# Last block of a two-layer network: the order of the last token tiles' matmuls, and a last store in three parts on two queues

## The chip, the core and the metric

The kernel runs on one core of a Trainium2 chip. The core has five engines that run their own instruction streams and meet at semaphores: TensorE (matmuls, with weight loads of their own), VectorE, ScalarE, GpSimd and SyncE (SP), which only issues transfers and waits. Sixteen DMA engines move data between the on-chip memory SBUF and the device's memory. TensorE writes to PSUM, another on-chip memory, in banks of 2 KB for each of 128 partitions; VectorE and ScalarE read PSUM, and DMA cannot, so a result goes from PSUM through a copy to SBUF and from there by a transfer to the output.

The metric is the device time of one execution in microseconds (us), lower is better. Of the kernel before there are three timed runs, and one more execution that the hardware profiler recorded.

## What is computed

```python
def _attn_ref(x, filt_r, filt_i):            # x: 8 x 3008 x 256
    X = np.fft.rfft(x, axis=1)
    F = (filt_r + 1j * filt_i)[None, :, :]
    y = np.fft.irfft(X * F, n=x.shape[1], axis=1)
    return y.astype(np.float32)

def _moe_ref(x, w_in, w_out, alpha):         # x: 24064 x 256, w_in: 256 x 2048
    h = x @ w_in
    g = np.maximum(h, 0.0) + alpha * np.minimum(h, 0.0)
    return (g @ w_out).astype(np.float32)    # w_out: 2048 x 256
```

A Fourier filter over each of 8 sequences, then for each of the 24064 tokens a network of two layers with a slope per hidden channel for negative values. The output is fp32, 256 values a token.

## The kernel before

The tokens are taken two sequences at a time, 6016 tokens, in twelve blocks of 512 tokens (one of them 384); in all there are 48 blocks. The Fourier work of the next sequences is put between the blocks' matmuls by a plan of steps written out by hand, and it is over before the last blocks, so that the end of the kernel is the two-layer network alone.

For a block, `Block.up` (L416) does the first layer. The hidden width of 2048 is split into 16 inner tiles of 128. For each inner tile two matmuls of 512 columns fill one bank of an `hps` tile in PSUM (L421). After each second inner tile ScalarE copies both to SBUF as fp16 (L427), and VectorE makes the slope in three instructions (L430 twice, L431); the result, `gtb`, is the weight of the second layer.

`Block.down` (L434) does the second layer. The block's 512 tokens are four token tiles of 128. For each token tile 16 matmuls, one for each inner tile `k`, accumulate 128 x 256 results into one half of an `op` tile (one bank of PSUM): the weight is the 128 x 128 piece of `gtb`, the moving operand `wout_s[:, k]`, 256 columns (L440). The token tiles run one after another, `k` from 0 to 15 in each. After every second token tile ScalarE copies both halves to an `osb` tile in SBUF (L445), and `store` (L395) issues a transfer from SP for each token tile, one part or two parts, because the tokens lie in the output in groups of 376 that the Fourier step has reordered (L403). The three `osb` tiles are used in turn, the two `op` tiles and the two `hps` tiles likewise.

The main loop (L511 to L520) runs the blocks with a lag: while block n does its first layer, four second-layer matmuls of block n - 1 follow each inner tile. After the loop the last block's second layer stands alone (L521, L522): 64 matmuls, in the order token tile 0 with `k` 0 to 15, then token tiles 1, 2 and 3. The last pair of inner tiles, `k` 14 and 15, comes from the last first-layer matmuls, through ScalarE and VectorE. In the last block token tile 0 is stored in one transfer, token tile 1 in two, token tiles 2 and 3 in one each.

Every transfer that SP and ScalarE issue uses one of eight semaphores in turn. At the end SP waits for each of them, and then the engines meet at a barrier.

Of the kernel before, what the change touches and what calls it, by code (L numbers as in the profile page):

```python
# [11 lines left out]
FP32 = mybir.dt.float32  # L12
# [3 lines left out]
N2 = 64  # L16
NK1 = 24
D = 256
# [14 lines left out]
AF = mybir.ActivationFunctionType  # L33
# [42 lines left out]
def kernel(  # L76
# [10 lines left out]
    nc = tc.nc  # L87
# [16 lines left out]
    p_osb = ctx.enter_context(tc.tile_pool(name="p_osb", bufs=3))  # L104
    psH = ctx.enter_context(tc.tile_pool(name="psH", bufs=2, space=bass.MemoryType.PSUM))
    psO = ctx.enter_context(tc.tile_pool(name="psO", bufs=2, space=bass.MemoryType.PSUM))
# [18 lines left out]
    wout_s = konst.tile([128, 16, D], FP16, name="wout_s")  # L125
# [215 lines left out]
    for q in range(2):  # L341
        nc.gpsimd.dma_start(
            out=wout_s[:, 8 * q : 8 * q + 8],
            in_=moe_w_out[1024 * q : 1024 * q + 1024].rearrange("(j p) d -> p j d", p=128))
# [44 lines left out]
    for p in range(NB // 2):  # L389
        t = 0  # L390
# [1 line left out]
            blocks.append((p, t, tn, 2 * p + (n >= 6)))  # L392
            t += tn

    def store(p, t0, osb, lane):  # L395
        t = t0
        while t < t0 + 128:
            b, r = 2 * p + t // NFFT, t % NFFT
            blk, o = r // 376, r % 376
            n = min(t0 + 128 - t, 376 - o)  # L400
            g, h = blk // 2, blk % 2
            row = b * NFFT + (o // 8) * N2 + NH * h + 8 * g
            nc.sync.dma_start(  # L403
                out=bass.AP(tensor=out.tensor, offset=out.offset + row * D,
                            ap=[[N2 * D, n // 8], [D, 8], [1, D]]),
                in_=osb[t - t0 : t - t0 + n, lane])
            t += n

    turn = [0]
# [1 line left out]
    class Block:  # L411
# [22 lines left out]
        def down(self, q):  # L434
            n = self.tn // 128
            for w in range(n * q, n * (q + 1)):
                si, k = w // 16, w % 16
                if si % 2 == 0 and k == 0:
                    self.op = psO.tile([128, 2, D], FP32, name="op")
                nc.tensor.matmul(self.op[:, si % 2], self.gts[k][:, 128 * si : 128 * si + 128],  # L440
                                 wout_s[:, k], start=(k == 0), stop=(k == 15))
                if k == 15 and (si % 2 == 1 or si == n - 1):
                    m = si % 2 + 1
                    osb = p_osb.tile([128, 2, D], FP32, name="osb")
                    nc.scalar.activation(osb[:, 0:m], self.op[:, 0:m], AF.Copy)  # L445
                    for lane in range(m):
                        store(self.p, self.t0 + 128 * (si - m + 1 + lane), osb, lane)

    plan = {}

# [37 lines left out]
    for b in range(3, NB):  # L488
        p = 96 * (b - 1)
# [19 lines left out]
    prev = None  # L509
    step = 0  # L510
    for p, t0, tn, _ in blocks:  # L511
# [6 lines left out]
                prev.down(j)  # L518
            step += 1
        prev = blk  # L520
    for q in range(16):  # L521
        prev.down(q)  # L522
    assert not plan


# [28 lines left out]
```

## Time and profile before

| what | value |
|---|---|
| timed runs, median of 3 | 797.27 us (796.84 to 797.43) |
| profiled execution, its time | 795.65 us |
| its span, first to last record | 793.9 us |
| TensorE busy in the span | 775.0 us, 98% |
| ScalarE, VectorE busy | 75%, 78% |
| DMA engines, mean share of the two data queues | 32.9% and 24.3% |
| granted TensorE clock, mean | 0.999 |

In the profile's lines an engine's name stands for its own work (PE is TensorE, PEld its weight loads, DVE VectorE, ACT ScalarE, POOL GpSimd, SP SyncE), and a q behind it for its queue, where it issues a transfer or waits. `out<-in` names what is written and read by the program's names, and L440 is a line of the kernel. A group's line has the count behind an x, then busy time and the mean of one in ns, then the idle time before, with what ended most of it. A timeline's line has the start and the length in us, and instructions of one line that follow each other stand together. Matmuls are pipelined: each is recorded with its whole way through the array, so that neighbours overlap, and the spacing of their starts is what one costs in a row. A transfer's issue is recorded on the queue of the engine that issues it; its landing is what a later wait is released by.

### The profile page before, as it was taken

How to read it: one execution, taken by the hardware profiler on the slowest of the kernel's cores; microseconds unless marked ns; L12 is line 12 of the kernel's file. 1: busy time of each engine (PE TensorE's matmuls, PEld its weight loads, DVE VectorE, ACT ScalarE, POOL GpSimd, SP SyncE). 2: the span in 40 equal slices, each digit the busy share in tenths (PEclk: the TensorE clock that was granted, in tenths of full speed). 3: DMA queues.
4: the chain of work that ended last, by engine and by line, in shares of the span. 5: the costliest groups of instructions: out<-in, count | busy, mean ns of one | idle time of the engine just before them, and what ended most of it. 6: DMA issues, size and time to landing. Idle time of an engine off the chain costs nothing.

```text
span 793.9 us, 16103 instructions
## 1 busy us (share of the span) xinstructions
PE 775.0 (98%) x5956; PEld 538.5 (68%) x5956; DVE 621.2 (78%) x1377; ACT 596.9 (75%) x836; POOL 193.2 (24%) x269
## 2 busy tenths in 40 slices
PE   7999999999999999999999999999999999999997
PEld 6756656666677666766667666766667766766665
DVE  4797985788788787888787877887878888777773
ACT  3788678878778887788768887688867777787663
POOL 7510441153123221341223311242212222000000
PEclk9999999999999999999999999999999999999999
DMA  9967557695776648574684657656494333511111
GB/s 187 209 142 194 115 112 175 192 180 118 150 173 113 138 102 192 123 147 101 149 189 82 135 120 167 152 109 139 101 212 90 66 77 81 138 36 28 41 40 54
DMA packets 102310, 100.58 MB, mean 127 GB/s; under 512 B 11320, under 2 KB 92744, under 8 KB 102104
## 3 DMA queue, kind: packets, MB, share of 16 engines
q1 hardware_dynamic: 79512, 68.80, 32.9%
q0 software_dynamic: 22720, 30.75, 24.3%
q8 instruction: 47, 0.77, 0.4%
q14 instruction: 31, 0.25, 0.1%
HBM read 56.26 MB, written 46.66 MB: 130 GB/s over the span
## 4 chain that ended last, share of the span: by engine, by line
PE 89%; ACT 4%; DMA 3%; DVE 2%; issue 1%; SPq 0%; POOL 0%; ACTq 0%; DVEq 0%; POOLq 0%
PE hps L421 38%; PE op L440 38%; PE psF L177 3%; PE psF L238 3%; ACT gtb L427 2%; PE psF L216 2%; PE psF L197 2%; DMA uu<-ww 1%; DMA filt_s<-in_filt_i_dram 1%; DMA xs<-in_x_dram 1%; ACT asb L245 1%; PE hps L288 1%; PE psF L317 1%; DMA v_dram<-v 0%; DMA zt<-v_dram 0%
## 5 line engine op out<-in xcount | busy, mean ns | idle before, releaser
L427 ACT ACTIVATE gtb<-hps 128x1024 f16<-128x1024 f32 (+1 forms) x384 | 385.4, 1005 | 133.3 <-PE hps L421 127.9
L440 PE MATMUL op<-wout_s,gtb 128*128 128x256 f16 x3008 | 451.1, 272 | 0.6 <-DVE gtb L431 0.6
L421 PE MATMUL hps<-yT,win_s 128*128 128x512 f16 (+1 forms) x1536 | 449.2, 374 | 0.4 <-ACT gtb L427 0.2
L440 PEld LDWEIGHTS <-gtb 128*128 128x128 f16 x3008 | 293.2, 98 | 189.6 <-DVE gtb L431 0.9
L430 DVE TENSOR_SCALAR m<-gtb,alm_s 128x512 f16<-128x512 f16 (+1 forms) x768 | 235.7, 349 | 126.7 <-ACT gtb L427 124.4
L431 DVE TENSOR_TENSOR gtb<-gtb,m 128x1024 f16<-128x1024 f16 (+1 forms) x384 | 261.6, 681 | 19.9
L203 POOL DMA_DIRECT2D uu<-ww x168 | 140.6, 980 | 438.3 <-PE hps L421 322.1
L421 PEld LDWEIGHTS <-win_s 128*128 128x128 f16 x1536 | 145.3, 98 | 30.9 <-issue 3.1
L245 ACT ACTIVATE asb<-psF 96x512 f16<-96x512 f32 x112 | 66.2, 591 | 11.5 <-PE psF L177 11.4
L245 ACT ACTIVATE yT<-psF 128x376 f16<-128x376 f32 x120 | 57.1, 485 | 13.3 <-PE psF L238 12.8
L445 ACT ACTIVATE osb<-op 128x512 f32<-128x512 f32 x96 | 56.1, 585 | 6.1 <-issue 3.2
L245 ACT ACTIVATE v<-psF 128x512 f16<-128x512 f32 x84 | 49.4, 595 | 10.8 <-PE psF L216 10.0
L200 DVE TENSOR_TENSOR ww<-psF,filts_s 128x512 f16<-128x512 f32 x84 | 57.4, 684 | 0.0
L201 DVE TENSOR_TENSOR uu<-psF,filt_s 128x512 f16<-128x512 f32 x84 | 57.2, 681 | 0.0
L139 POOL DMA_DIRECT2D xs<-in_x_dram x64 | 43.9, 946 | 25.8 <-PE psF L177 15.0
L177 PE MATMUL psF<-xs,wf_s 94*96 94x512 f16 x112 | 42.7, 381 | 1.5 <-ACT v L245 1.0
L238 PE MATMUL psF<-wi_s,zt 96*128 96x94 f16 x504 | 40.3, 205 | 1.9 <-DMA zt<-v_dram 1.0
L238 PEld LDWEIGHTS <-zt 96*128 96x128 f16 x512 | 34.3, 97 | 6.2 <-issue 1.5
L216 PE MATMUL psF<-uu,twi_s 128*128 128x256 f16 x168 | 31.3, 273 | 2.3 <-ACT yT L245 0.9
L197 PE MATMUL psF<-at,twf_s 128*128 128x256 f16 x168 | 32.1, 273 | 0.3 <-ACT asb L245 0.2
L216 PEld LDWEIGHTS <-twi_s 128*128 128x128 f16 x168 | 15.7, 98 | 5.9 <-DMA uu<-ww 2.7
L197 PEld LDWEIGHTS <-twf_s 128*128 128x128 f16 x168 | 15.8, 98 | 2.8 <-DVE uu L201 0.7
(55 smaller groups left out, 173.3 us busy)
## 6 DMA issues: line engine op xcount, KB each, us to landing
out_dram<-osb SPq DMA_DIRECT2D x128, 128.0 KB
xs<-in_x_dram POOLq DMA_DIRECT2D x64, 188.0 KB, 5.4
a_dram<-asb SPq DMA_DIRECT2D x28, 384.0 KB
uu<-ww POOLq DMA_DIRECT2D x168, 64.0 KB, 2.9
v_dram<-v SPq DMA_DIRECT2D x112, 96.0 KB
zt<-v_dram SPq DMA_DIRECT2D x28, 384.0 KB
at<-a_dram SPq DMA_DIRECT2D x20, 384.0 KB
at<-a_dram SPq DMA_DIRECT2D x32, 96.0 KB
```

Source lines behind the costliest of these rows:

```text
L177: nc.tensor.matmul(ps[0:96], wf1_s, xs[:, o : o + 512], start=True, stop=True)
L197: nc.tensor.matmul(px[:, kh], twf_s[:, k1], self.at[:, k1], start=True, stop=True)
L200: nc.vector.tensor_mul(ww, px, filts_s[:, 2 * kp : 2 * kp + 2])
L203: nc.gpsimd.dma_start(out=uu[o : o + 64], in_=ww[64 - o : 128 - o], accum_op=OP.add)
L216: nc.tensor.matmul(pv[:, kh], twi_s[:, k1], u[:, kh], start=u is us[0], stop=u is us[-1])
L238: nc.tensor.matmul(ps[:, m], self.zt[:, 8 * g + 4 * mh + m, dh * 128 : dh * 128 + 128], wi3_s, start=True, stop=True)
L245: nc.scalar.activation(o, i, AF.Copy)
L421: nc.tensor.matmul(self.hps[:, j % 2, 0:tn], win_s[:, kt, j * 128 : (j + 1) * 128], yT[:, kt, self.t0 : self.t0 + tn], start=(kt == 0), st ...
L427: nc.scalar.activation(g[:, :, 0:tn], self.hps[:, :, 0:tn], AF.Copy)
L430: nc.vector.tensor_scalar(m[:, i, 0:tn], g[:, i, 0:tn], 0.0, a, OP.min, OP.mult)
L431: nc.vector.tensor_add(g[:, :, 0:tn], g[:, :, 0:tn], m[:, :, 0:tn])
L440: nc.tensor.matmul(self.op[:, si % 2], self.gts[k][:, 128 * si : 128 * si + 128], wout_s[:, k], start=(k == 0), stop=(k == 15))
```

## The change

A method `finish` takes the place of the last block's 16 calls of `down`, and `store` learns to take another queue and a range of columns.

```diff
-    def store(p, t0, osb, lane):
+    def store(p, t0, osb, lane, eng=nc.sync, ca=0, cb=D):
...
-            nc.sync.dma_start(
-                out=bass.AP(tensor=out.tensor, offset=out.offset + row * D,
-                            ap=[[N2 * D, n // 8], [D, 8], [1, D]]),
-                in_=osb[t - t0 : t - t0 + n, lane])
+            eng.dma_start(
+                out=bass.AP(tensor=out.tensor, offset=out.offset + row * D + ca,
+                            ap=[[N2 * D, n // 8], [D, 8], [1, cb - ca]]),
+                in_=osb[t - t0 : t - t0 + n, lane, ca:cb])
...
+        def finish(self):
+            def down(acc, si, k, first, ca=0, cb=D):
+                nc.tensor.matmul(acc, self.gts[k][:, 128 * si : 128 * si + 128], wout_s[:, k, ca:cb],
+                                 start=first, stop=(k == 15), skip_group_check=True)
+
+            op = psO.tile([128, 2, D], FP32, name="op")
+            osb = p_osb.tile([128, 2, D], FP32, name="osb")
+            for ks in (range(14), range(14, 16)):
+                for si in range(2):
+                    for k in ks:
+                        down(op[:, si], si, k, si == 0 and k == 0)
+            nc.scalar.activation(osb, op, AF.Copy)
+            for lane in range(2):
+                store(self.p, self.t0 + 128 * lane, osb, lane)
+            osb = p_osb.tile([128, 2, D], FP32, name="osb")
+            parts = ((0, 0, 256, nc.sync), (1, 0, 128, nc.scalar), (1, 128, 256, nc.sync))
+            accs = [psH.tile([128, 2, 512], FP32, name="hps")[:, 0] for _ in range(2)]
+            accs.insert(0, psO.tile([128, 2, D], FP32, name="op")[:, 0])
+            for (lane, ca, cb, eng), acc in zip(parts, accs):
+                acc = acc[:, 0 : cb - ca]
+                for k in range(16):
+                    down(acc, 2 + lane, k, k == 0, ca, cb)
+                nc.vector.tensor_copy(osb[:, lane, ca:cb], acc)
+                store(self.p, self.t0 + 256 + 128 * lane, osb, lane, eng, ca, cb)
...
-    for q in range(16):
-        prev.down(q)
+    prev.finish()
```

Token tiles 0 and 1 now share the order: `k` 0 to 13 of token tile 0, `k` 0 to 13 of token tile 1, then `k` 14 and 15 of each. ScalarE copies both as before, and SP stores them in three transfers as before. Token tile 2 is accumulated by itself, copied by VectorE and stored from SP. Token tile 3 is done twice over half the columns: 16 matmuls of 128 columns, a copy on VectorE, a store from ScalarE's queue; then the other 16, a copy, a store from SP. The three accumulators lie in an `op` tile and in the two `hps` tiles, which the first layer no longer needs. Each half of token tile 3 loads the 16 weights again.

The program's instructions before the last block's second layer are the same, engine by engine. TensorE has 16 matmuls and 16 weight loads more, VectorE three copies more, ScalarE one copy less and one transfer to issue, and SP's last transfer has half the size.

## The prediction

> **What bounds the kernel now.** I read the page first, its spans and its chain.
>
> ```profile
> span 793.9 us, 16103 instructions
> PE 775.0 (98%) x5956; PEld 538.5 (68%) x5956; DVE 621.2 (78%) x1377; ACT 596.9 (75%) x836; POOL 193.2 (24%) x269
> ...
> PE 89%; ACT 4%; DMA 3%; DVE 2%; issue 1%; SPq 0%; POOL 0%; ACTq 0%; DVEq 0%; POOLq 0%
> ```
>
> TensorE is busy for 98% of the span. The change touches nothing before the last block's second layer, so only the end matters: the last 14 us. I take it from the timeline of that stretch, in windows cut so that single stores stand alone.
>
> ```profile
> 780.49 2.13 PE L440 MATMUL op<-wout_s,gtb 128*128 128x256 f16 x18
> 782.46 0.69 DVE L431 TENSOR_TENSOR gtb<-gtb,m 128x1024 f16<-128x1024 f16 x1
> 782.99 1.51 SPq L403 DMA_DIRECT2D out_dram<-osb  x2
> 783.21 5.63 PE L440 MATMUL op<-wout_s,gtb 128*128 128x256 f16 x50 [0.60 <-DVE gtb L431]
> 785.44 0.60 ACT L445 ACTIVATE osb<-op 128x512 f32<-128x512 f32 x1 [3.24 <-issue]
> 786.06 2.07 SPq L403 DMA_DIRECT2D out_dram<-osb  x3
> 788.93 0.60 ACT L445 ACTIVATE osb<-op 128x512 f32<-128x512 f32 x1 [2.90 <-PE op L440]
> 789.55 0.57 SPq L403 DMA_DIRECT2D out_dram<-osb  x1
> 789.55 1.20 SPq L403 DMA_DIRECT2D out_dram<-osb  x2
> ```
>
> The columns are start, length, engine, line. The 18 matmuls that end at 782.62 are the previous block's last 4 and the first 14 of token tile 0. Matmul 15 needs inner tile 14, whose last VectorE step runs from 782.46 to 783.15. TensorE stands still from 782.62 to 783.21, then does the other 50 in 5.63 us, one each (5.63 - 0.27)/49 = 0.109 us, to 788.84. ScalarE copies token tiles 2 and 3 in one piece (788.93 to 789.53), and SP issues their two stores, the second from 790.2. What follows is in the waits of SP's queue and in the view of line 403:
>
> ```profile
> SPq L549 <- DMA out_dram<-osb: 1.7, 1, 1.7
> ...
> L403 SPq DMA_DIRECT2D out_dram<-osb x248: 447/632/1817, 60.5 to 790.2; - x124
> ```
>
> SP has issued by 789.55 + 1.20 = 790.75 and waits 1.7 us, to about 792.5, for the last store to land: 2.35 us after that store's issue began at 790.17. From there to 793.9 it is closing waits and the barrier, 1.4 us, which stay. So the end is a chain of links: the stall, the matmuls, a copy, two issues in a row, a landing.
>
> **The change part by part.**
>
> *Order of the matmuls.* Token tile 1's first 14 now stand between tile 0's 14 and the two that need the last inner tiles. They take 14 x 0.109 = 1.53 us, so TensorE asks for inner tile 14 at 782.62 + 1.53 = 784.15; it is ready at 783.15. The stall is covered with 1.0 us to spare. Token tiles 0 and 1 end at 782.62 + 18 x 0.109 = 784.59; before, it was 783.21 + 0.27 + 17 x 0.109 = 785.34. Gain **0.75**: the gap of 0.59, and 0.16 because the first matmul after a gap takes its whole 0.27 and not 0.109. Putting both tiles in one bank with one start flag changes no time.
>
> *Half-width matmuls.* Token tile 3's 16 matmuls of 256 columns become 32 of 128, with 16 weight loads more. Nearest rows: 128x128 matmuls with a fresh weight load each, at full clock, and the weight load of this very layer.
>
> ```profile
> 18.43 0.22 PE L306 MATMUL op<-gtb,ww 128*128 128x128 f16 x1 [1.12 <-DVE gtb L355]
> ...
> 18.77 0.22 PE L306 MATMUL op<-gtb,ww 128*128 128x128 f16 x1
> ...
> 33.70 0.61 PE L351 MATMUL op<-id 128*128 128x128 f16 x8
> ...
> L440 PEld LDWEIGHTS <-gtb 128*128 128x128 f16 x3008 | 293.2, 98 | 189.6 <-DVE gtb L431 0.9
> ```
>
> Between 18.43 and 18.77 lie six steps, 0.057 us each; the run of eight gives (0.61 - 0.22)/7 = 0.056. Two halves thus cost 0.112 against 0.109: 16 x 0.003 = 0.05 us lost, and the last, shorter matmul leaves the array 0.05 sooner. I take **0**. The other bound is a load that isn't hidden: 32 x (0.098 - 0.056) = 1.3 us lost. The rows with a load per matmul are the same shape, so I stay with them. TensorE ends at 784.59 + 32 x 0.109 = 788.08 less 0.01.
>
> *The copies.* Before: one ScalarE copy of 0.60, begun 0.09 after TensorE. After: three on VectorE, which has nothing left to do. No row shows this copy; the nearest are VectorE's reads of PSUM.
>
> ```profile
> L248 DVE CAST gtb<-hps 128x384 f16<-128x384 f32 x8 | 4.2, 554 | 10.2 <-PE hps L267 10.1
> L248 DVE CAST at<-psF 128x512 f16<-128x512 f32 x1 | 0.7, 692 | 0.3 <-PE psF L278 0.3
> L364 DVE COPY al_s<-op 128x16 f32<-128x16 f32 x1 | 0.2, 175 | 0.0
> ...
> 14.18 0.80 PE L278 MATMUL psF<-id,gtb 128*128 128x128 f16 x8
> 15.02 0.69 DVE L248 CAST at<-psF 128x512 f16<-128x512 f32 x1 [0.35 <-PE psF L278]
> ```
>
> One more column costs (692 - 554)/128 = 1.08 ns, so 128 columns take 554 - 256 x 1.08 = 278 ns, and 256 take 416. VectorE began 15.02 - 14.98 = 0.04 after TensorE. On the path stands only the last copy: 0.04 + 0.28 = 0.32 instead of 0.09 + 0.60 = 0.69. Gain **0.37**; bounds 0.47 (as short as the 16-column row, 0.175) and 0.23 (as long as 256 columns). The first VectorE copy gains a wait for the stores that read its buffer three turns ago, those of the previous block's token tiles 0 and 1; SP had issued that block's later stores by 784.50, and the copy starts at 786.4. Behind it on VectorE are only the other two copies.
>
> *The issues.* The three stores of tiles 0 and 1 now follow the ScalarE copy that ends at 784.59 + 0.09 + 0.60 = 785.28, take 2.07, and hold SP until 787.36. Tile 2 is copied by 784.59 + 16 x 0.109 + 0.04 + 0.42 = 786.79 but is issued behind them, 787.41 to 787.98. The first half of tile 3 is copied at 787.50 and goes to ScalarE's queue, where nothing stands before or behind it. The second half: TensorE 788.07, copy done 788.39, SP free since 788.03, issue at **788.41**. If the two queues cannot issue at once, three issues in a row, 0.62 apart as the pair at 789.55 shows, put the last at 788.64. I take 788.5. Before it was 790.17: 1.67 us sooner, of which 0.75 is the stall, 0.37 the copy and 0.62 the one issue that no longer stands ahead, less 0.07 for waiting.
>
> The Trainium skill, Perfetto Trace Analysis, section on the HWDGE DMA instruction, says that the descriptor generator is one block, locked by the sequencer that uses it; by that rule the issue is at 788.64, 0.14 later than I take. No row of this trace has two such queues.
>
> *The landing.* The last store is 64 KB in 512-byte pieces, not 128 KB in 1-KB pieces. The views of the DMA engines, in 40 slices, first the two last stores (789.5 to 792.7), then four stores of 96 KB in 512-byte pieces (677 to 679.6):
>
> ```profile
> GB/s 0 0 0 0 0 0 0 0 0 0 0 0 0 0 0 38 141 179 154 218 333 230 244 77 128 141 192 205 282 307 205 141 51 13 0 0 0 0 0 0
> ...
> GB/s 0 0 0 0 0 0 0 0 0 0 0 0 0 32 118 213 228 213 213 173 197 166 166 236 205 205 205 181 213 174 173 221 213 205 221 173 418 182 181 228
> ```
>
> Both run near 200 GB/s, so 512-byte pieces aren't slower per byte, and 64 KB move in 0.33 us instead of 0.65. The landing shortens from 2.35 to **2.03**. Bounds: 2.35 (no gain), and 1.76, the first DMA of the program, 32 KB, issued at 0.75 and awaited by TensorE until 2.51:
>
> ```profile
> 0.75 0.36 SPq L320 DMA_DIRECT2D id<-c_id  x1
> ...
> 2.51 1.78 PE L351 MATMUL op<-id 128*128 128x128 f16 x15 [2.51 <-DMA id<-c_id]
> ```
>
> **The sum.** 1.67 + 0.32 = 1.99; I round down to **1.95 us**, since an interleaved store from the other queue can hold some pieces up. Ends: 1.53 (issue at 788.64, landing 2.35) and 2.35 (issue at 788.41, landing 1.76). The profiled execution itself took 795.65, 1.62 under the median of the timed runs; it becomes 793.70, and the median 797.27 becomes **795.32**, likeliest case's own range 794.8 to 795.8.
>
> **The rivals.**
>
> *Halving saves nothing (chance 0.13).* A store's time may be fixed cost: the first slice with traffic begins at 789.5 + 15 x 0.08 = 790.7, 1.15 us after its issue, and the last ends at 792.2, 0.3 before SP is released. With the landing at 2.35 and the issues strictly one after another, the gain is 1.53: 795.74. Against it: the 0.65 us of traffic per store that the slices show. The Trainium skill, DMA: Bandwidth & Descriptors, Rules for kernel authors, speaks for it: under 64 KB a transfer is mostly overhead, and issuing from several engines saves the time of the issue alone. Here the traffic is 0.65 of the store's 2.35 us, so the row agrees that most is overhead, not that all is.
>
> *A third queue costs outside the span (0.13).* The page knows two queues for data:
>
> ```profile
> q1 hardware_dynamic: 79512, 68.80, 32.9%
> q0 software_dynamic: 22720, 30.75, 24.3%
> ```
>
> Between span and execution lie 795.65 - 793.9 = 1.75 us. If these two queues make that up, a third adds 0.9, and the gain shrinks to 1.05: 796.2. Nothing in the trace says what the 1.75 us are.
>
> *Weight loads pace the half-width matmuls (0.06).* The 1.3 us above come back: 796.6. Against it stand the rows at 0.056; for it, that none is a run of 32.
>
> *Slower: the first store on ScalarE's queue lands late (0.06).* That queue has carried nothing. On the two others the first transfer took 1.76 us (SP) and, on the POOL queue, which the chain shows at the start:
>
> ```profile
> 1.26 2.19 POOL xs L139 x4
> 3.45 6.13 DMA xs<-in_x_dram
> ```
>
> With such 6.1 us after its four issues, the half tile issued at 787.5 to 788.1 lands at 794.2, 1.7 us after the present last landing at 792.5: 799.0. It decides the time from the point where this landing takes over 3 us from issue, and makes the kernel slower from 5.0. Against it: that transfer was 188 KB from memory at the start, beside others; SP's first was as quick as any.
>
> *The change doesn't do what it says:* the stall stays, if the last inner tile came after 784.15. It has 1.0 us of cover; I give that no chance of its own.
>
> **How the numbers follow.** My forecast has 0.62, the rivals 0.13, 0.13, 0.06 and 0.06. About 0.2% (1.6 us) can be told from no change. The forecast passes that line by 0.35 us and its own range crosses it, so I count nine tenths of it as faster and half of the first rival: 0.62. The second and third rivals are within 0.2%, and so is what is left: 0.33. The last gives 0.05 slower. The range runs from 794.7 (gain 2.35, and 0.2 for the scatter of the medians) to 797.0, which takes in the first three rivals.
>
> **What would show it.** After: no wait of TensorE for line 431 at the end; the 32 half-width matmuls at 0.056; copies on VectorE of 0.42, 0.28 and 0.28; SP's last issue near 788.5 counted from the same start, ScalarE's at 787.5; the waits of SP's queue of about 1.4 us behind the last issue; a span near 791.9. Wrong would be the forecast if half-width matmuls run at 0.1, if ScalarE's issue or landing comes last, or if the span is shorter by 2 us and the execution is not.

## The result and the profile after

The changed kernel takes 794.80 us (median of 13 runs, 793.34 to 797.12); the kernel before, run beside it, 796.84 us (13 runs, 795.49 to 799.30). The medians differ by 2.04 us; the ratio taken over all runs is 0.9977, 95% interval 0.9966 to 0.9988, which is 1.8 us or 0.23% less, with 1.0 to 2.7 us in the interval. The profiled execution took 794.64 us, its span is 792.8.

The span fell by 1.1 us only, so the first question is where the two executions differ. The view by windows gives, for each stretch, its length, TensorE's busy time with the number of matmuls, the granted clock, the DMA share and GB/s. Before:

```profile
0.00:200.00 200.00, 187.28 (x1563) 1.00 0.76 162
200.00:780.00 580.00, 579.44 (x4325) 1.00 0.52 116
```

After:

```profile
0.00:200.00 200.00, 187.15 (x1555) 1.00 0.75 161
200.00:780.00 580.00, 579.44 (x4325) 1.00 0.52 116
```

From 200 us on, both run the same 4325 matmuls in the same time. In the first 200 us the changed kernel did eight fewer, which puts everything later by about 1 us, in a stretch where the two programs are the same. So a span compares two openings as well as two endings. The endings are compared by the **tail**: from the end of the last VectorE step of the last block (line 431) to the end of the span. Before it is 793.884 - 783.156 = 10.73 us (the row of that step is in the prediction). After, in the timeline:

```profile
783.56 0.69 DVE L431 TENSOR_TENSOR gtb<-gtb,m 128x1024 f16<-128x1024 f16 x1
783.98 3.44 PE L451 MATMUL op<-wout_s,gtb 128*128 128x256 f16 x30
785.76 0.60 ACT L460 ACTIVATE osb<-op 128x512 f32<-128x512 f32 x1 [2.47 <-issue]
787.26 1.95 PE L451 MATMUL hps<-wout_s,gtb 128*128 128x128 f16 x32
787.46 0.42 DVE L471 COPY osb<-op 128x256 f32<-128x256 f32 x1 [3.21 <-PE op L451]
788.35 0.29 DVE L471 COPY osb<-hps 128x128 f32<-128x128 f32 x1 [0.47 <-PE hps L451]
788.53 0.57 SPq L403 DMA_DIRECT2D out_dram<-osb  x1
788.67 0.65 ACTq L403 DMA_DIRECT2D out_dram<-osb  x1
789.24 0.29 DVE L471 COPY osb<-hps 128x128 f32<-128x128 f32 x1 [0.60 <-PE hps L451]
789.56 0.55 SPq L403 DMA_DIRECT2D out_dram<-osb  x1
...
SPq L573 <- DMA out_dram<-osb: 1.3, 2, 0.9
```

The tail is 792.82 - 784.25 = **8.57 us, 2.16 less**. The matmuls run on through the end of line 431 without a gap; the row of TensorE waiting for it is gone. TensorE ends at 789.21, 4.96 us after that step (before: 5.69). The last copy is done 0.33 after TensorE, not 0.69. The last issue comes 5.31 after the step, not 7.01. The last row is the waits of SP's queue: after its last issue, over at 790.11, SP waits 0.9 us for ScalarE's store and then 0.4 for its own. The landings themselves are in the trace's semaphore records, finer than these rounded waits: the last store has landed by 791.54, 1.98 after the start of its issue (before: 792.54, 2.37 after). Here and below a landing is counted from the start of the issue.

### The profile page after: what moved, and what is told of

Same layout as the page of the kernel before. It is cut to its first block, busy times and chain, and to the rows that moved or that the text cites. A ratio compares the mean times of both kernels' runs of the same rounds, so it can differ in the third digit from the quotient of the medians.

```text
span 792.8 us, 16142 instructions
## 1 busy us (share of the span) xinstructions
PE 775.8 (98%) x5972; PEld 540.2 (68%) x5972; DVE 622.5 (79%) x1380; ACT 596.4 (75%) x835; POOL 193.0 (24%) x269
## 4 chain that ended last, share of the span: by engine, by line
PE 89%; ACT 3%; DMA 3%; DVE 2%; issue 1%; POOL 1%; SPq 0%; ACTq 0%; POOLq 0%
PE hps L421 38%; PE op L440 38%; PE psF L177 3%; PE psF L238 3%; PE psF L216 2%; PE psF L197 2%; ACT gtb L427 2%; DMA xs<-in_x_dram 1%; DMA uu<-ww 1%; PE hps L288 1%; PE op L451 1%; ACT asb L245 1%; DVE m L430 1%; PE psF L317 1%; DVE ww L200 1%
## 5 line engine op out<-in xcount | busy, mean ns | idle before, releaser
L440 PE MATMUL op<-wout_s,gtb 128*128 128x256 f16 x2944 | 444.0, 272 | 0.0
L440 PEld LDWEIGHTS <-gtb 128*128 128x128 f16 x2944 | 287.0, 98 | 188.0
```

## The experiments

All tails are from one profiled execution each; a tail does not contain the opening. How far they scatter can be read from a link that several kernels share: the last 64-KB store, when SP issues it with no other issue running, lands after 1.98, 1.99, 1.99, 1.99 and 2.00 us in five of them. "The changed kernel" is the kernel after.

**Only the new order of token tiles 0 and 1.** Token tiles 2 and 3 are done as before, and the loop over the parts goes:

```diff
-            parts = ((0, 0, 256, nc.sync), (1, 0, 128, nc.scalar), (1, 128, 256, nc.sync))
...
+            op = psO.tile([128, 2, D], FP32, name="op")
+            for lane in range(2):
+                for k in range(16):
+                    down(op[:, lane], 2 + lane, k, k == 0)
+            nc.scalar.activation(osb, op, AF.Copy)
+            for lane in range(2):
+                store(self.p, self.t0 + 256 + 128 * lane, osb, lane)
```

> Only the new order of token tiles 0 and 1; token tiles 2 and 3 as before (one ScalarE copy, two SP stores). Measured by the tail, from the end of the last VectorE step of line 431 to the end of the span: 10.73 us before, 8.57 after. Links add up: the stall and its refill go, 0.73 us, nothing else: tail 10.00, TensorE ends 4.96 after that step instead of 5.69, copy 0.60 and two issues 0.62 apart unchanged. Rival, the stall alone is the gain and the parts give back what they save: tail 8.6. Rival, the stall moves elsewhere (another wait for VectorE): tail 10.7.

Measured, in its timeline (start, length, engine, line):

```profile
784.21 5.84 PE L451 MATMUL op<-wout_s,gtb 128*128 128x256 f16 x52
784.44 0.69 DVE L431 TENSOR_TENSOR gtb<-gtb,m 128x1024 f16<-128x1024 f16 x1
786.64 0.60 ACT L460 ACTIVATE osb<-op 128x512 f32<-128x512 f32 x1 [2.47 <-issue]
790.14 0.60 ACT L468 ACTIVATE osb<-op 128x512 f32<-128x512 f32 x1 [2.90 <-PE op L451]
```

The 52 matmuls run through the end of line 431 in one piece, and TensorE ends 4.92 after it. Tail 795.08 - 785.13 = 9.95, 0.78 less than before, where 0.73 was expected. Its timed ratio, 0.9994 (0.9978 to 1.0009), is too wide to tell 0.78 us (0.1%) from nothing.

**Only the parts and the second queue.** Token tiles 0 and 1 in the old order:

```diff
-            for ks in (range(14), range(14, 16)):
+            for ks in (range(16),):
```

> Only the three parts and the second queue; token tiles 0 and 1 in the old order, one after the other. Links add up: TensorE stalls 0.59 again, and the copy, the issue and the landing keep their gain, 2.16 - 0.73 = 1.43 us: tail 9.30. Rival, the stall alone is the gain: tail 10.7.

```profile
785.51 0.69 DVE L431 TENSOR_TENSOR gtb<-gtb,m 128x1024 f16<-128x1024 f16 x1
786.26 3.89 PE L451 MATMUL op<-wout_s,gtb 128*128 128x256 f16 x34 [0.60 <-DVE gtb L431]
789.98 1.95 PE L451 MATMUL hps<-wout_s,gtb 128*128 128x128 f16 x32
791.97 0.29 DVE L471 COPY osb<-hps 128x128 f32<-128x128 f32 x1 [0.60 <-PE hps L451]
```

In its timeline the wait of 0.60 is back. Tail 795.56 - 786.20 = 9.36, 1.37 less than before (ratio 0.9983, 0.9968 to 0.9998). The two halves of the change give 0.78 and 1.37, together 2.15 of the whole's 2.16: they add up, and neither gives back what the other saves.

**How much cover the stall needs.** Only 3 of token tile 1's matmuls stand ahead of token tile 0's last two:

```diff
-            for ks in (range(14), range(14, 16)):
-                for si in range(2):
-                    for k in ks:
-                        down(op[:, si], si, k, si == 0 and k == 0)
+            for si, ks in ((0, range(14)), (1, range(3)), (0, range(14, 16)), (1, range(3, 16))):
+                for k in ks:
+                    down(op[:, si], si, k, si == 0 and k == 0)
```

> The changed kernel with only 3 of token tile 1's matmuls ahead of token tile 0's last two, instead of 14. Theory, the stall is covered matmul by matmul, 0.109 us each, and 7 would do for all of it: tail 9.36 (without cover) - 3 x 0.109 = 9.03, a wait of 0.27 left before TensorE's next matmul. Rival, any work in between hides it: tail 8.57. Rival, a gap costs the same however short: tail 9.36.

```profile
785.52 0.69 DVE L431 TENSOR_TENSOR gtb<-gtb,m 128x1024 f16<-128x1024 f16 x1
786.27 3.56 PE L451 MATMUL op<-wout_s,gtb 128*128 128x256 f16 x31 [0.27 <-DVE gtb L431]
```

Tail 795.25 - 786.22 = 9.03, and the wait in the timeline is 0.27: both as the theory has it. A stall is paid for in the time of the work put in front of it, 0.109 us a matmul here. At that price some seven matmuls would cover it all; that was not run, and the 14 of the change leave no wait.

**One queue.** The changed kernel with the first half stored from SP:

```diff
-            parts = ((0, 0, 256, nc.sync), (1, 0, 128, nc.scalar), (1, 128, 256, nc.sync))
+            parts = ((0, 0, 256, nc.sync), (1, 0, 128, nc.sync), (1, 128, 256, nc.sync))
```

> The changed kernel, but the first half of token tile 3 is stored from SP too. Links add up: three issues in a row from 4.28 after the last VectorE step, each 0.55 to 0.62, so the last half is issued at 5.50 instead of 5.31: tail 8.77, 0.2 longer. Rival, the second queue already waits for the first one's issue and saves nothing: tail 8.57.

```profile
783.76 0.69 DVE L431 TENSOR_TENSOR gtb<-gtb,m 128x1024 f16<-128x1024 f16 x1
788.56 0.29 DVE L471 COPY osb<-hps 128x128 f32<-128x128 f32 x1 [0.47 <-PE hps L451]
789.45 0.29 DVE L471 COPY osb<-hps 128x128 f32<-128x128 f32 x1 [0.60 <-PE hps L451]
...
788.74 0.57 SPq L403 DMA_DIRECT2D out_dram<-osb  x1
789.40 0.55 SPq L403 DMA_DIRECT2D out_dram<-osb  x1
790.04 0.56 SPq L403 DMA_DIRECT2D out_dram<-osb  x1
```

The last copy is done at 789.74, but SP issues its store only at 790.04, after the two others, 0.65 apart. Tail 793.32 - 784.46 = 8.86, 0.29 longer than with two queues (0.2 expected: three issues follow each other a little slower than I took). So the second queue does save time.

**No halves.** The changed kernel with token tile 3 at full width:

```diff
-            parts = ((0, 0, 256, nc.sync), (1, 0, 128, nc.scalar), (1, 128, 256, nc.sync))
-            accs = [psH.tile([128, 2, 512], FP32, name="hps")[:, 0] for _ in range(2)]
+            parts = ((0, 0, 256, nc.sync), (1, 0, 256, nc.sync))
+            accs = [psH.tile([128, 2, 512], FP32, name="hps")[:, 0] for _ in range(1)]
```

> The changed kernel, but token tile 3 is done at full width: 16 matmuls of 256 columns, one VectorE copy, one SP store of 128 KB. Links add up: the copy takes 0.42 instead of 0.29, the landing 2.35 instead of 1.98, TensorE ends 0.06 sooner: tail 9.0. Rival, a store's time is fixed and halving saves only in the copy: tail 8.65.

```profile
786.64 0.69 DVE L431 TENSOR_TENSOR gtb<-gtb,m 128x1024 f16<-128x1024 f16 x1
792.28 0.42 DVE L471 COPY osb<-hps 128x256 f32<-128x256 f32 x1 [1.32 <-PE hps L451]
792.74 0.55 SPq L403 DMA_DIRECT2D out_dram<-osb  x1
...
SPq L573 <- DMA out_dram<-osb: 1.7, 1, 1.7
```

The last issue comes 5.41 after the step, 0.10 later than with halves, and SP waits 1.7 us for its landing, 2.28 after the issue instead of 1.98. Tail 796.36 - 787.33 = 9.03, 0.46 longer. Of this, 0.10 is the later issue (the copy takes 0.13 longer, and TensorE ends 0.04 sooner) and 0.30 the landing. The last 0.06 is not the halving's: with one transfer fewer the last store has another semaphore, and one closing wait more follows it (below). The tail of 9.0 that was expected came out in part by luck, as the landing was 0.07 shorter than expected and the closing wait, which had not been counted, 0.06 longer. A store's time is not fixed.

**Is ScalarE's queue slow, or was it in the way of SP's?** ScalarE's store in the changed kernel took 0.65 to issue and landed 2.39 after it (788.67 to 791.06); SP's last store took 0.55 and 1.98. Both are 64 KB. First the queues exchanged, then both halves from ScalarE:

```diff
-            parts = ((0, 0, 256, nc.sync), (1, 0, 128, nc.scalar), (1, 128, 256, nc.sync))
+            parts = ((0, 0, 256, nc.sync), (1, 0, 128, nc.sync), (1, 128, 256, nc.scalar))
```

> The changed kernel with the two halves' queues exchanged: first half from SP, last half from ScalarE. In the changed kernel ScalarE's half took 0.65 to issue and 2.39 to land, SP's last half 0.55 and 1.98. Theory, overlap with another issue made it slow: here the last half overlaps SP's issue by 0.15 us only, lands some 2.05 after its issue: tail 8.6 to 8.7. Rival, ScalarE's queue is slower by itself: the last half lands 2.39 after its issue: tail 9.0.

```diff
-            parts = ((0, 0, 256, nc.sync), (1, 0, 128, nc.scalar), (1, 128, 256, nc.sync))
+            parts = ((0, 0, 256, nc.sync), (1, 0, 128, nc.scalar), (1, 128, 256, nc.scalar))
```

> The changed kernel with both halves stored from ScalarE's queue; SP has long issued token tile 2 when the last half comes. Theory, overlap made it slow: the last half is issued alone, 0.55, and lands in 1.98: tail 8.57. Rival, ScalarE's queue is slower by itself: landing 2.39, tail 9.0.

The issues, in the timelines; with the queues exchanged:

```profile
789.24 0.55 SPq L403 DMA_DIRECT2D out_dram<-osb  x1
789.62 0.66 ACTq L403 DMA_DIRECT2D out_dram<-osb  x1
```

and with both halves from ScalarE, after token tile 2 from SP:

```profile
787.43 0.56 SPq L403 DMA_DIRECT2D out_dram<-osb  x1
787.57 0.66 ACTq L403 DMA_DIRECT2D out_dram<-osb  x1
788.46 0.56 ACTq L403 DMA_DIRECT2D out_dram<-osb  x1
```

ScalarE's issue takes 0.65 to 0.66 beside one of SP's and 0.56 alone (788.46). That store, issued alone, lands after 2.01, as SP's do; in the exchanged kernel, with an overlap of 0.17, it lands after 2.10. Tails 8.70 and 8.61, where 9.0 would have shown a slower queue: ScalarE's queue is no slower by itself.

That the overlap is what makes it slow is not shown. The issue is longer by the same 0.1 whether 0.43 or 0.17 of SP's issue is still to run, SP's own issues in these overlaps stay at 0.55 to 0.57, and in every kernel the issue of 0.65 to 0.66 is also the first transfer on ScalarE's queue, while the one of 0.56 is its second. A price of a queue's first use fits as well, and no run has a first issue that stands alone. The landing is 0.4 later behind a 128-KB store issued 0.14 before it, and 0.1 later behind a 64-KB store issued 0.38 before it; whether that arises in the issue or because both stores' data moves at the same time (in the changed kernel ScalarE's pieces from 790.19 to 790.71, the 128-KB store's up to 790.52), these runs do not tell. The first half of token tile 3 has that time to spare.

**The closing waits.** At the end SP waits for eight semaphores one after another. In the changed kernel the last store has the second of them, so that the other six come after it. Six small transfers more at the start move it to the last:

```diff
-    nc.sync.dma_start(out=wi3_s, in_=wi3_d.ap())
+    for r in range(0, 96, 14):
+        nc.sync.dma_start(out=wi3_s[r : min(r + 14, 96)], in_=wi3_d.ap()[r : min(r + 14, 96)])
```

> The changed kernel with the constant wi3_s loaded in seven transfers at the start instead of one, so that the last store falls on the last of the eight semaphores that SP waits for in turn, not on the second. Theory: after the last landing SP now passes six waits fewer, 0.062 us each: tail 8.57 - 0.37 = 8.20. Rival, the closing time is the barrier's and SP's waits lie beside it: tail 8.57.

```profile
783.94 0.69 DVE L432 TENSOR_TENSOR gtb<-gtb,m 128x1024 f16<-128x1024 f16 x1
789.05 0.66 ACTq L404 DMA_DIRECT2D out_dram<-osb  x1
789.62 0.29 DVE L472 COPY osb<-hps 128x128 f32<-128x128 f32 x1 [0.60 <-PE hps L452]
...
SPq L574 <- DMA out_dram<-osb: 0.8, 2, 0.4
```

Its lines stand one further down. Up to the last copy all is where it was (5.68 after the start of the last VectorE step in both kernels). The wait for the landings falls from 1.3 to 0.8, because SP passes the other semaphores before the data is there. Tail 792.86 - 784.63 = 8.23, 0.35 less than the changed kernel. Timed, its ratio to the kernel before is 0.9971 (0.9955 to 0.9988; median 794.41 against 796.24): it beats the kernel before, and the changed one by its tail; the timed runs alone can't tell these two apart. The four timed kernels stand in the order of their tails: the new order alone, the parts alone, the whole change and this one are 0.06, 0.17, 0.23 and 0.29% faster by their ratios, and their tails are shorter by 0.10, 0.17, 0.27 and 0.31% of the time.

**A smaller last part.** The kernel of the last experiment, with token tile 3 cut at column 192:

```diff
-            parts = ((0, 0, 256, nc.sync), (1, 0, 128, nc.scalar), (1, 128, 256, nc.sync))
+            parts = ((0, 0, 256, nc.sync), (1, 0, 192, nc.scalar), (1, 192, 256, nc.sync))
```

> The kernel of e8_lane7 (tail 8.23) with token tile 3 cut into 192 and 64 columns instead of 128 and 128: the last store is 32 KB in 256-byte pieces. Links add up, if TensorE keeps 0.44 ns a column: the last copy falls by 64 columns, 0.07, the landing from 2.00 by the traffic of 32 KB at 200 GB/s, 0.16: tail 8.00. Rival, small matmuls and small pieces cost as much as large ones: 64-column matmuls at 0.056 like 128-column ones put TensorE's end 0.45 later, and 256-byte pieces land no sooner: tail 8.6.

```profile
786.20 0.69 DVE L432 TENSOR_TENSOR gtb<-gtb,m 128x1024 f16<-128x1024 f16 x1
789.89 1.95 PE L452 MATMUL hps<-wout_s,gtb 128*128 128x192 f16 x32
791.19 0.57 SPq L404 DMA_DIRECT2D out_dram<-osb  x1
791.80 0.66 ACTq L404 DMA_DIRECT2D out_dram<-osb  x1
791.88 0.22 DVE L472 COPY osb<-hps 128x64 f32<-128x64 f32 x1
792.13 0.55 SPq L404 DMA_DIRECT2D out_dram<-osb  x1
```

Neither theory. The 32 matmuls take the same 1.95 us, so those of 64 columns keep the pace per column, and the copy falls to 0.22: the last issue comes 5.25 after the step, 0.07 sooner. But the landing takes 2.16 instead of 2.00, and the tail is 795.21 - 786.89 = 8.32, 0.09 longer than with halves. The loss is not in the issue. SP's issue before had ended at 791.76 when ScalarE's began, and that one took 0.66 all the same; SP's last issue began 0.33 before ScalarE's ended, and took only 0.55. So here the second of two overlapping issues is not the longer one. What is left is what comes behind the issue: ScalarE's 96 KB, issued 0.33 earlier, are moved at the same time (its pieces from 793.13 to 793.75, the last store's from 793.46 to 793.87), and the pieces have 256 bytes; this run does not tell the two apart.

## Why the prediction was right, step by step

- *The time.* Forecast 795.32 in a range of 794.7 to 797.0, measured 794.80, near the lower end. Most of the miss is the base: the kernel before had 797.27 in three runs and 796.84 in the thirteen of the comparison, and between the medians 2.04 us lie where 1.95 were forecast. Single runs scatter by 4 us, twice the gain, so that the median fell inside so narrow a range is in part luck; the tails and their links test the mechanism.
- *The stall.* Predicted 0.75 from the gap and its refill; alone it gave 0.78. In the whole change TensorE ended 0.73 sooner; with token tile 3 at full width it ended 0.77 sooner, so the halves cost 0.04. The partial cover shows that the mechanism is the cover.
- *Half-width matmuls at nothing.* 32 in 1.95 us are (1.95 - 0.22)/31 = 0.056 us each, as in the rows they were taken from (TensorE's end came 0.04 later all the same: the prediction set the shorter last matmul, out 0.05 sooner, against the slower pace, but the last of two halves also starts some 0.05 later). The rival of unhidden weight loads is out.
- *The copies.* 0.42, 0.29 and 0.29 against 0.42, 0.28 and 0.28, begun 0.04 after TensorE. It is the size more than the engine that saves: ScalarE's four copies of 256 columns in the kernel before take 0.378 each, VectorE's took 0.424. Halves copied by ScalarE were not run.
- *The issues.* Counted from the last VectorE step I had taken 788.5 - 783.15 = 5.35; it was 5.31. The forecast for the case that the two queues can't issue at once, 5.49, did not come: SP's issue ran from 788.53 to 789.10 and ScalarE's from 788.67 to 789.33. The Trainium skill's rule in Perfetto Trace Analysis, section on the HWDGE DMA instruction, that the generator is locked for one sequencer, does not show in these rows as a lock for the whole issue: ScalarE's issue is 0.10 us longer than alone, while 0.43 of SP's was still to run. Whether the 0.10 is a shorter lock or the first use of the queue is open.
- *The landing.* Predicted 2.03, measured 1.98. The first rival (halving saves nothing) expected 2.35; token tile 3 at full width shows what that is worth, 0.30 (2.28 to 1.98). The other 0.09 of the difference from 2.37 goes with the store ahead, issued 0.62 before the last one in the kernel before and 1.12 before it at full width; that was not tested by itself.
- *The third queue* costs 0.05 us at most outside the span: 794.64 - 792.82 = 1.82 there, against 795.65 - 793.88 = 1.77, and 1.77 in the profiled run with the new order alone, which has no such queue. *Its late first store* did not decide: it landed 2.39 after its issue, where about 2.9 would have been needed.
- *The sum.* I rounded 1.99 down to 1.95 for pieces that could hold each other up; the tail gave 2.16, and nothing showed of pieces that hold the last store up. The 0.17 above the 1.99 have three parts: the issue came 1.70 sooner instead of 1.67, the landing shortened by 0.39 instead of 0.32, and the time from the last landing to the end, which I had taken to stay, went from 1.35 to 1.28. This last is a term that the sum did not have: the last store's semaphore moved from the first to the second of the eight, one wait of 0.06 less.
- *What went wrong beside it* is the check by the span. I expected 791.9 and 793.70 for the profiled execution, as if its opening repeated itself; it came out at 792.8 and 794.64, because TensorE was 1.1 us later at the last block. Over the eleven profiles of this study the last VectorE step ends anywhere between 783.14 and 787.33, and the difference arises in the first 200 us. Two views of the windows show it, token tile 3 at full width (783.16 + 4.17) and both halves from ScalarE (783.16 - 0.02):

```profile
0.00:200.00 200.00, 186.24 (x1535) 0.97 0.74 159
200.00:780.00 580.00, 579.44 (x4324) 1.00 0.53 117
```

```profile
0.00:200.00 200.00, 186.01 (x1563) 1.00 0.76 162
200.00:780.00 580.00, 579.44 (x4325) 1.00 0.52 116
```

The first has 28 matmuls fewer by 200 us and a granted clock of 0.97 there; the second has as many as the kernel before. The clock is not all of it: the kernel with three matmuls of cover had 22 fewer by then (1541) at a clock of 1.00. What else makes the openings differ stays open. After 200 us all are alike. The line of 0.2% was drawn from three runs that lay within 0.6 us; thirteen lie within 4.

## What to carry to other kernels

When TensorE is busy to the end, the time behind it is a chain of copy, issue, landing and closing waits, and each link is priced by its own row: cut the last piece small, give it an engine that is free for the copy and a queue without an issue ahead of it, and fill the wait for the last input with work that is ready, as much of it as the wait is long. Smaller is not always better: a last part of a quarter gained nothing over a half. And where a change is worth a microsecond in eight hundred, compare the profiles from the last event that both share, not their spans.

## What the runs showed of the hardware that was not expected

SP and ScalarE can have transfers in issue at the same time (788.53 to 789.10 and 788.67 to 789.33). ScalarE's issue then took 0.65 us instead of 0.56, and its data landed up to 0.4 later (2.39 against 2.01); whether by the overlap, by the other store's data or by the queue's first use is open. SP's waits on finished semaphores cost about 0.06 us each when they stand behind the last landing (0.35 for six), so which semaphore the last transfer gets was worth as much here as halving its data (0.30 in the landing).
